# Two heads of batch 0 taken by query block, their probabilities split into float16 pairs and transposed by DMA

## The chip, the core and the metric

The kernel runs on one core of one Trainium2 chip. The metric is device time in microseconds (us) of one execution, the median of the runs. Engines are named as in the profile: PE is TensorE, PEld its weight loads, DVE is VectorE, ACT is ScalarE, POOL is GpSimd, SP is SyncE, which only issues DMAs here.

## What is computed

Four batches of eight heads of clustered attention, and behind it a feed-forward network with the Mish function on all 3072 tokens. The reference, cut:

```python
def _attn_ref(q, k, v, centroids):          # q, k, v: 4 x 8 x 768 x 64, centroids: 8 x 16 x 64
    scale = 1.0 / np.sqrt(D)
    q_assign = np.argmax(np.einsum('bhsd,hcd->bhsc', q_n, c_n), axis=-1)   # q, k, c normalised
    k_assign = np.argmax(np.einsum('bhsd,hcd->bhsc', k_n, c_n), axis=-1)
    mask = q_assign[:, :, :, None] == k_assign[:, :, None, :]
    scores = np.where(mask, scale * np.matmul(q, k.transpose(0, 1, 3, 2)), -1000000000.0)
    attn = np.exp(scores - np.max(scores, axis=-1, keepdims=True))
    attn = attn / (np.sum(attn, axis=-1, keepdims=True) + 1e-09)
    return np.matmul(attn, v)

def _moe_ref(x, w_in, w_out):                # x: 3072 x 512, w_in: 512 x 2048, w_out: 2048 x 512
    h = x @ w_in
    g = h * np.tanh(softplus(h))             # Mish
    return g @ w_out
```

## The kernel before

**Units.** Attention is cut into 96 units: a head g (0 to 31, eight to a batch) and a query block of 256 rows. Before, unit i is head i // 3, block i % 3. A unit has two halves `a` of 128 query rows, and two units in a row, 2m and 2m + 1, are a pair m, whose product with the values shares one PSUM bank.

**Steps of a half.** `scores` makes 128 x 768 scores on TensorE in one of two PSUM buffers; `rowmax` (VectorE) their row maximum, `expo` (ScalarE) the exponentials with their sum, `total` and `recip` the reciprocal of the sum. From there two ways are in use. In the f32 way (`mode` 3, units below `T["wide"]`, which is 24: all of batch 0), `p_lo` transposes the exponentials on TensorE into PSUM (tile `q`, six transposes), `ptrans` copies the halves of it to SBUF, one on ScalarE and one on VectorE; `pv` multiplies them, three parts, with the raw f32 values (`vraw`) and brings the reciprocals into the same bank; `pv_out` scales them on ScalarE (`rb`), multiplies on VectorE (`xf`), and splits the result into two float16 parts on ScalarE and GpSimd. In the float16 way (all later units), `p_hi` writes the high float16 part of the scaled probabilities (tile `hl`), `p_lo` on VectorE the low part, `ptrans` is one DMA transpose of both from the SP queue, `pv` is 36 float16 matmuls, and `pv_out` (ScalarE) with `x_lo` (VectorE) writes the two parts of x.

**Values.** For the float16 way `v_high` (GpSimd) and `v_split` (VectorE) make float16 pairs of the values, for two heads at a time.

**Operands of the scores.** For each head, `prep_hi` and `prep_lo` on GpSimd make `A` and `B` from the loaded `qk`, and `copy_t`, `copy_z`, `copy_b`, `copy_a` and `hot_copy` move halves of them and of the cluster rows between partitions, most by DMA: `T` from A, `Z` from B, then B's upper half from T. Each of A, B, T and Z has two buffers, so the operands of head n take those of head n - 2.

**Feed-forward network.** For a token block of 256 rows and a slice f of 256 of the 2048 columns there is a step j (24 to a batch): `m1` makes h (two halves of 12 matmuls each), `e_mish` applies Mish on ScalarE, for two j with one change of activation tables to it and one back, `e_gh` and `e_gl` make float16 pairs, and `m2` adds into the output. `m1` of a token block needs x of all eight heads for that block.

**Order.** Nothing is reordered when the program runs: each engine runs its instructions in the order in which they were written. `Plan` sorts all operations by a place on an axis counted in units (the tables `T` and `N`) and lets each pull the ones it needs ahead of itself:

```python
    def at(self, t, fn, *args):
        op = fn.__name__, *args
        self.ops[op] = (t + SHIFT.get(op, 0), len(self.ops), fn, args)
```

`SHIFT`, which moves single operations, is empty before.

Of the kernel before, what the change touches and what calls it, by code (L numbers as in the profile page):

```python
# [72 lines left out]
def tile_clustered_attention_mish_ffn(  # L73
# [61 lines left out]
    units = [(g, qb, g) for g in range(B * H) for qb in range(3)]  # L135
    NG = units[-1][2] + 1
# [295 lines left out]
    def v_high(b, hp):  # L432
        pl.after(scaled(b), ("v_load", b, hp))
        t = vst[b, hp, "raw"]
        if b == 0 and T["wide"] >= 24:
            return
# [214 lines left out]
    def expo(i, a):  # L651
        pl.after(("rowmax", i, a))
        p = pp.tile([P, S], F32, tag="p", name=f"p{i}_{a}")
        if mode(i, a) != 3:
            l = sm.tile([P, 1], F32, tag="l", name=f"l{i}_{a}", bufs=10)
        else:
            if a == 0:
                st["l", i] = sm.tile([P, 2], F32, tag="ll", name=f"l{i}", bufs=5)
            l = st["l", i][:, a : a + 1]
# [116 lines left out]
    def pv_out(i):  # L776
        pl.after(("pv", i // 2, 2))
        g, qb, _ = units[i]
        b, h = divmod(g, H)
        if mode(i, 0) == 3:  # L780
            pl.after(("v_scale", b))
# [34 lines left out]
    def m1(j, fi):  # L816
# [3 lines left out]
        if fi == 0:  # L820
# [11 lines left out]
    def e_mish(j):  # L832
        pl.after(("m1", j, 0), ("m1", j, 1))
# [241 lines left out]
    def ffn(j):  # L1075

        return T["ffn"] + j
# [24 lines left out]
    for n in range(NG):  # L1102
        for op, key in (
# [9 lines left out]
            else:  # L1113
                pl.at(start(first[n]) + T[key] * (3 if n else 1), op, n)
# [166 lines left out]
    'v_sqd': -5.865,  # L1281
    'cent_put': -16.698,
    'ffn': 23.993,
    'w_f': 0.342,
    'w_q': 0.827,
    'w_lo': 0.312,
    ('z', 'prep_hi'): -17.672,
    ('z', 'prep_lo'): -12.698,
    ('z', 'copy_t'): -15.888,
    ('z', 'copy_a'): -14.732,  # L1290
    ('z', 'copy_b'): -14.765,
    ('z', 'copy_z'): -16.337,
    ('z', 'assign_mm'): -11.552,
    ('z', 'assign_turn'): -14.554,
    ('z', 'assign_max'): -16.003,
    ('z', 'assign_hot'): -13.258,
    ('z', 'assign_back'): -12.666,
    ('z', 'assign_put'): -12.998,
    ('z', 'hot_direct'): -6.027,
    ('z', 'assign_stg'): -14.77,  # L1300
    ('z1', 'prep_hi'): -15.822,
    ('z1', 'copy_t'): -0.562,
    ('z1', 'prep_lo'): -2.335,
    ('z1', 'copy_z'): 2.134,
    ('z1', 'copy_b'): 2.571,
    ('z1', 'copy_a'): 1.339,
    'as_turn': 2.548,
    'as_max': -0.442,
    'as_hot': 2.486,
    'as_back': 0.39,  # L1310
    'as_put': 0.846,
    'as_stg': 1.187,
    'n_late': 9,
    'wide': 24,
    'v_s0': 36.503,
    'act_q': 3,
# [72 lines left out]
    ('w_s', 0): 0.187,
    ('w_s', 1): -0.515,  # L1390
# [88 lines left out]
```

## Time and profile before

| | |
|---|---|
| median of 3 runs | 879.22 us (878.64 to 881.77) |
| the profiled execution | 880.14 us, its span 878.4 us |
| PE busy | 843.7 us, 96% of the span |
| PEld busy | 609.1 us, 69% |
| DVE busy | 701.5 us, 80% |
| ACT busy | 521.9 us, 59% |
| POOL busy | 436.1 us, 50% |
| granted clock of PE | full in all of the 40 slices |

The span runs from the first to the last instruction, and the profiled execution's time has 1.7 us around it. A busy share is a mean over stretches with different limits: the stretches are to be read one by one. Matmuls overlap, so the time that a group of them holds TensorE is read from the start of the first to the start of what follows, not from their durations.

### The profile page before, as it was taken

How to read it: one execution, taken by the hardware profiler on the slowest of the kernel's cores; microseconds unless marked ns; L12 is line 12 of the kernel's file. 1: busy time of each engine (PE TensorE's matmuls, PEld its weight loads, DVE VectorE, ACT ScalarE, POOL GpSimd, SP SyncE). 2: the span in 40 equal slices, each digit the busy share in tenths (PEclk: the TensorE clock that was granted, in tenths of full speed). 3: DMA queues.
4: the chain of work that ended last, by engine and by line, in shares of the span. 5: the costliest groups of instructions: out<-in, count | busy, mean ns of one | idle time of the engine just before them, and what ended most of it. 6: DMA issues, size and time to landing. Idle time of an engine off the chain costs nothing.

```text
span 878.4 us, 17434 instructions
## 1 busy us (share of the span) xinstructions
PE 843.7 (96%) x6670; PEld 609.1 (69%) x6671; DVE 701.5 (80%) x1178; ACT 521.9 (59%) x881; POOL 436.1 (50%) x410
## 2 busy tenths in 40 slices
PE   7989789979999999999999999999999999999998
PEld 3766566757677767677676766776776777777787
DVE  6889988889888789788888788788888776488831
ACT  5777877666555656557456566475574565346520
POOL 1453656587575546567566447466575543110000
PEclk9999999999999999999999999999999999999999
DMA  9755672288678998788579898997777876000001
GB/s 343 218 164 141 198 221 59 72 152 166 128 138 178 190 181 156 162 158 173 118 138 189 199 157 143 165 175 143 134 148 139 141 134 121 13 1 13 1 26 36
DMA packets 253060, 121.51 MB, mean 138 GB/s; under 512 B 230288, under 2 KB 230800, under 8 KB 252976
## 3 DMA queue, kind: packets, MB, share of 16 engines
q1 hardware_dynamic: 247632, 108.46, 58.5%
q10 hardware_dynamic: 5344, 11.93, 6.3%
q8 instruction: 53, 0.87, 0.4%
q14 instruction: 31, 0.25, 0.1%
HBM read 35.72 MB, written 6.29 MB: 48 GB/s over the span
## 4 chain that ended last, share of the span: by engine, by line
PE 71%; DVE 12%; DMA 6%; ACT 6%; issue 3%; POOL 2%; ACTq 0%; SPq 0%; POOLq 0%; DVEq 0%
PE o L751 9%; PE h L828 8%; PE h L830 7%; PE h L829 7%; PE O L869 7%; PE O L871 7%; PE O L870 7%; PE s L631 5%; PE s L636 5%; DVE m L648 3%; ACT p L660 2%; DMA T<-A 2%; DVE hl L715 2%; DMA stage<-in_w_out_dram 1%; PE as L543 1%
## 5 line engine op out<-in xcount | busy, mean ns | idle before, releaser
L660 ACT ACTIVATE p<-s,m 128x768 f32<-128x768 f32 x192 | 172.8, 900 | 157.7 <-DVE l L672 77.2
L698 POOL TENSOR_SCALAR hl<-p,l 128x768 f16<-128x768 f32 x144 | 174.8, 1214 | 135.9 <-DVE l L680 68.8
L648 DVE TENSOR_REDUCE m<-s 128x1 f32<-128x768 f32 x192 | 182.8, 952 | 37.9 <-PE s L636 34.0
L828 PE MATMUL h<-x,w 128*128 128x256 f16 x640 | 175.8, 275 | 3.7 <-ACT u L839 3.7
L829 PE MATMUL h<-x,w 128*128 128x256 f16 x640 | 174.4, 273 | 0.0
L830 PE MATMUL h<-x,w 128*128 128x256 f16 x640 | 174.4, 273 | 0.0
L715 DVE SCALAR_TENSOR_TENSOR hl<-p,l,hl 128x768 f16<-128x768 f32 x144 | 166.8, 1159 | 7.7 <-POOL hl L698 7.5
L631 PE MATMUL s<-A,B 128*128 128x384 f32 x384 | 119.2, 391 | 8.9 <-ACT p L660 6.8
L853 DVE SCALAR_TENSOR_TENSOR g<-u,mscg,g 128x512 f16<-128x512 f32 x80 | 93.6, 1170 | 38.6 <-POOL g L845 38.3
L869 PE MATMUL O<-w,g 128*128 128x512 f16 x320 | 121.7, 380 | 0.0
L871 PE MATMUL O<-w,g 128*128 128x512 f16 x320 | 121.3, 379 | 0.0
L870 PE MATMUL O<-w,g 128*128 128x512 f16 x320 | 121.3, 379 | 0.0
L845 POOL TENSOR_SCALAR g<-u,mscg 128x512 f16<-128x512 f32 x80 | 74.2, 930 | 71.7 <-ACT u L839 55.1
L636 PE MATMUL s<-Z,T 80*128 80x384 f32 x384 | 99.0, 339 | 1.0 <-DVE T L603 1.0
L828 PEld LDWEIGHTS <-w 128*128 128x128 f16 x768 | 75.1, 98 | 31.8 <-issue 20.6
L829 PEld LDWEIGHTS <-w 128*128 128x128 f16 x768 | 75.5, 98 | 15.2 <-issue 4.0
L830 PEld LDWEIGHTS <-w 128*128 128x128 f16 x768 | 75.1, 98 | 8.7
L751 PE MATMUL o<-pt,v 128*64 128x256 f16 x1296 | 78.4, 274 | 1.6 <-DMA pt<-hl 1.3
L631 PEld LDWEIGHTS s<-A,B 128*128 128x128 f32 x384 | 61.1, 190 | 25.1 <-ACT p L660 10.5
L751 PEld LDWEIGHTS <-v 128*64 128x64 f16 x1296 | 68.1, 110 | 11.9 <-issue 9.3
L636 PEld LDWEIGHTS s<-Z,T 80*128 80x128 f32 x384 | 69.7, 189 | 1.3 <-ACT Z L600 1.3
L839 ACT ACTIVATE u<-h,msch 128x512 f32<-128x512 f32 x80 | 51.8, 685 | 16.8 <-PE h L830 12.5
(225 smaller groups left out, 1313.4 us busy)
## 6 DMA issues: line engine op xcount, KB each, us to landing
qk<-in_qk_dram SPq DMA_DIRECT2D x32, 384.0 KB, 4.8
stage<-in_w_in_dram SPq DMA_DIRECT2D x16, 512.0 KB, 7.7
stage<-in_w_out_dram SPq DMA_DIRECT2D x16, 512.0 KB, 4.5
vraw<-in_vP_dram SPq DMA_DIRECT2D x16, 384.0 KB, 6.1
T<-A ACTq DMA_DIRECT2D x30, 192.0 KB, 2.9
Z<-B SPq DMA_DIRECT2D x30, 192.0 KB, 2.9
B<-T ACTq DMA_DIRECT2D x28, 192.0 KB, 4.1
out_dram<-osb SPq DMA_DIRECT2D x20, 256.0 KB, 3.0
```

Source lines behind the costliest of these rows:

```text
L631: nc.tensor.matmul(s[:, j, :384], st["B", n][:, q0 : q0 + P], st["A", n][:, j * 384 : (j + 1) * 384], start=True, stop=False,)
L636: nc.tensor.matmul(s[:, j, :384], st["T", n][: D + NCL, q0 : q0 + P], st["Z", n][: D + NCL, j * 384 : (j + 1) * 384], start=False, stop=True,)
L648: nc.vector.tensor_reduce(m, st["s", i, a][:, :, :384], axis=AX.XY, op=ALU.max, negate=True)
L660: nc.scalar.activation(p.rearrange("p (n x) -> p n x", n=2), st["s", i, a][:, :, :384], AF.Exp, bias=st["m", i, a], scale=1.0, accum_out=l,)
L715: nc.vector.scalar_tensor_tensor(t[:, 1], p, r, t[:, 0], op0=ALU.mult, op1=ALU.subtract)
L751: nc.tensor.matmul(o[s * D : s * D + D, :256], v if early else v[:, int(part == 1)], st["pt", 2 * m + s][:, :, c + (0 if early or part < 2 ...
L828: nc.tensor.matmul(o, wh, xh, start=(c == 0), stop=False)
L829: nc.tensor.matmul(o, wh, xl, start=False, stop=False)
L830: nc.tensor.matmul(o, wl, xh, start=False, stop=(c == 3))
L869: nc.tensor.matmul(o, gh, wh, start=(f == 0 and fi == 0), stop=False)
L870: nc.tensor.matmul(o, gh, wl, start=False, stop=False)
L871: nc.tensor.matmul(o, gl, wh, start=False, stop=(f == 7 and fi == 1))
```

## The change

`T["wide"]` goes from 24 to 18: units 18 to 23, heads 6 and 7 of batch 0, take the float16 way. With `f_hi` of the first 24 units at 0, their `p_hi` is on ScalarE. The six units are put in another order, so that the two heads alternate by query block; the values of these two heads (`hp` 3) get their float16 pair. `ffn` places the first feed-forward steps two units sooner, and lets this shrink to nothing at step 24. `hold` moves the operand steps of heads 7 and 8 back by 0.84 units. New terms in `after` keep the order of halves. The tables get new numbers, and `SHIFT` an entry for most operations up to unit 31.

```diff
+    units[18:24] = [(g, qb, g) for qb in range(3) for g in (6, 7)]
...
     def v_split(b, hp):
         pl.after(("v_high", b, hp))
-        if b == 0 and T["wide"] >= 24:
+        if b == 0 and hp < T["wide"] // 6:
             return
...
     def ffn(j):
 
-        return T["ffn"] + j
+        return T["ffn"] + j - T["lead"] * max(0, 1 - j / 24)
...
-                pl.at(start(first[n]) + T[key] * (3 if n else 1), op, n)
+                pl.at(start(first[n]) + T[key] * (3 if n else 1) + T["hold"].get(n, 0), op, n)
...
+    'lead': 2,
+    'hold': {7: 0.838, 8: 0.844},
...
-    'wide': 24,
+    'wide': 18,
...
 SHIFT = {
-   
+    ('p_lo', 19, 0): 0.589, ('recip', 25, 1): -0.052, ('w_hi', 11): 6.904, ('assign_hot', 2): 2.97,
```

What it does to the order, at three places. In the names below the first number is the unit (for `A`, `B`, `T`, `Z` and `qk` the head), the second the half, and the last one only counts buffers. First VectorE around units 18 and 19, before:

```order
L727 COPY pt17_1682<-q17_1_3_1712 128x384
L678 RECIPROCAL l17_1621<-l17_1621 128x2
L648 TENSOR_REDUCE m18_1_1738<-s18_1_1721 128x1
L727 COPY pt18_1748<-q18_0_3_1744 128x384
L648 TENSOR_REDUCE m19_0_1770<-s19_0_1761 128x1
L727 COPY pt18_1748<-q18_1_3_1776 128x384
L678 RECIPROCAL l18_1719<-l18_1719 128x2
L796 TENSOR_TENSOR xf2_1_1506<-o8_1728,rb16_1803 64x256
L796 TENSOR_TENSOR xf2_2_1658<-o8_1728,rb16_1803 64x256
L648 TENSOR_REDUCE m19_1_1811<-s19_1_1797 128x1
```

The same place in the change:

```order
L730 COPY pt17_1690<-q17_1_3_1726 128x384
L683 RECIPROCAL l18_0_1734<-l18_0_1734 128x1
L649 TENSOR_REDUCE m18_1_1745<-s18_1_1740 128x1
L718 SCALAR_TENSOR_TENSOR hl18_0_1747<-p18_0_1733,l18_0_1734,hl18_0_1747 128x768
L649 TENSOR_REDUCE m19_0_1766<-s19_0_1761 128x1
L683 RECIPROCAL l18_1_1777<-l18_1_1777 128x1
L683 RECIPROCAL l19_0_1786<-l19_0_1786 128x1
L799 TENSOR_TENSOR xf2_1_1499<-o8_1752,rb16_1792 64x256
L799 TENSOR_TENSOR xf2_2_1668<-o8_1752,rb16_1792 64x256
L649 TENSOR_REDUCE m19_1_1805<-s19_1_1800 128x1
L718 SCALAR_TENSOR_TENSOR hl19_0_1807<-p19_0_1785,l19_0_1786,hl19_0_1807 128x768
L718 SCALAR_TENSOR_TENSOR hl18_1_1812<-p18_1_1776,l18_1_1777,hl18_1_1812 128x768
```

The copies of `q` have given way to `p_lo` (`hl`), twice as many reciprocals stand there, and the low parts of two halves stand together behind the row maximum of a later half. Next GpSimd at the operands of head 7, before:

```order
L672 TENSOR_SCALAR l17_1621<-l17_1621 128x2
L484 TENSOR_SCALAR qk7_839<-qk7_839,scq_138 128x768
L487 TENSOR_SCALAR A_7_1733<-qk7_839 128x768
L500 TENSOR_TENSOR B_7_1753<-qk7_839,A_7_1733 128x768
L337 TENSOR_SCALAR w9_997<-w9_997,ws1r_1702 128x1024
L340 TENSOR_SCALAR w8_796<-w9_997 128x1024
L672 TENSOR_SCALAR l18_1719<-l18_1719 128x2
```

and in the change:

```order
L485 TENSOR_SCALAR qk7_744<-qk7_744,scq_138 128x768
L488 TENSOR_SCALAR A_7_1635<-qk7_744 128x768
L501 TENSOR_TENSOR B_7_1648<-qk7_744,A_7_1635 128x768
L675 TENSOR_SCALAR l17_1629<-l17_1629 128x2
L802 TENSOR_TENSOR x0_2_0_1491<-xf2_0_1492,x0_2_0_1491 128x256
L675 TENSOR_SCALAR l18_0_1734<-l18_0_1734 128x1
L675 TENSOR_SCALAR l18_1_1777<-l18_1_1777 128x1
L338 TENSOR_SCALAR w9_993<-w9_993,ws1r_1712 128x1024
```

The three steps of head 7 stand one unit earlier, ahead of the sum of unit 17, and the sums of the two halves of unit 18 are apart. Last ScalarE at the first feed-forward steps, before:

```order
L660 ACTIVATE p25_0_2241,l25_0_2242<-s25_0_2193,m25_0_2198 128x768
L795 ACTIVATE rb22_2261<-o11_2153,vsp_484 128x256
L798 CAST x0_3_1_1958<-xf3_1_1959 128x256
L798 CAST x0_3_2_2089<-xf3_2_2090 128x256
L838 ACT_TABLE_LOAD
L839 ACTIVATE u0_2274<-h0_2126,msch0_2114 128x512
L839 ACTIVATE u1_2279<-h1_2205,msch0_2114 128x512
L841 ACT_TABLE_LOAD
L660 ACTIVATE p25_1_2282,l25_1_2283<-s25_1_2226,m25_1_2231 128x768
```

and in the change:

```order
L663 ACTIVATE p23_0_2076,l23_0_2077<-s23_0_2035,m23_0_2040 128x768
L843 ACT_TABLE_LOAD
L844 ACTIVATE u0_2089<-h0_1963,msch0_1900 128x512
L844 ACTIVATE u1_2092<-h1_2015,msch0_1900 128x512
L846 ACT_TABLE_LOAD
L515 DMA B_8_2031<-T_8_2064 64x768
L703 ACTIVATE hl22_1_2108<-p22_1_2059,l22_1_2060 128x768
L791 ACTIVATE x0_3_1_2149<-o10_2112 64x256
L663 ACTIVATE p23_1_2158,l23_1_2159<-s23_1_2081,m23_1_2086 128x768
```

The first two `e_mish` stand between the halves of unit 23 instead of those of unit 25, and a DMA of head 8 (`B` from `T`) is issued behind them.

## Rows read from the trace of the kernel before

**Rows 1.** Windows: us, busy of PE, PEld, DVE, ACT, POOL, clock, DMA, GB/s

```profile
0.00:127.50 127.50, 110.88 (x826) 75.23 (x827) 111.71 (x204) 95.99 (x184) 54.83 (x76) 1.00 0.69 214
127.50:163.00 35.50, 32.03 (x243) 22.74 (x241) 30.68 (x62) 26.41 (x54) 20.11 (x22) 1.00 0.30 82
163.00:207.00 44.00, 36.73 (x310) 28.06 (x308) 37.15 (x62) 29.26 (x48) 33.88 (x31) 1.00 0.67 132
207.00:350.00 143.00, 142.46 (x1126) 101.03 (x1126) 123.04 (x196) 86.87 (x144) 87.93 (x74) 1.00 0.82 162
```

**Rows 2.** Timeline of PE, units 21 and 22: start, us, what

```profile
147.40 0.88 PE L708 MATMUL q<-ident,p 128*128 128x128 f32 x6
148.03 0.59 PE L631 MATMUL s<-A,B 128*128 128x384 f32 x2
...
148.91 1.08 PE L751 MATMUL o<-pt,vraw 128*64 128x256 f32 x8
149.83 0.66 PE L763 MATMUL o<-ident,l 128*64 128x128 f32 x8
```

**Rows 3.** Timeline of PE, later places

```profile
169.67 0.28 PE L828 MATMUL h<-x,w 128*128 128x256 f16 x1
...
170.88 0.27 PE L830 MATMUL h<-x,w 128*128 128x256 f16 x1
...
204.93 2.16 PE L751 MATMUL o<-pt,v 128*64 128x256 f16 x36
207.01 0.63 PE L631 MATMUL s<-A,B 128*128 128x384 f32 x2
...
209.15 0.38 PE L869 MATMUL O<-w,g 128*128 128x512 f16 x1
...
209.80 0.38 PE L869 MATMUL O<-w,g 128*128 128x512 f16 x1
```

**Rows 4.** Groups of DVE, whole run: busy us, mean ns, idle before, releaser

```profile
L715 DVE SCALAR_TENSOR_TENSOR hl<-p,l,hl 128x768 f16<-128x768 f32 x144 | 166.8, 1159 | 7.7 <-POOL hl L698 7.5
L727 DVE COPY pt<-q 128x384 f32<-128x384 f32 x48 | 26.3, 549 | 4.1 <-PE q L708 3.9
L680 DVE RECIPROCAL l<-l 128x1 f32<-128x1 f32 x144 | 23.7, 164 | 4.9
```

**Rows 5.** One line's instructions (`p_lo`): duration ns min/median/max

```profile
L715 DVE SCALAR_TENSOR_TENSOR hl<-p,l,hl x144: 998/1018/2477, 173.0 to 740.2; 128x768 f16<-128x768 f32 x144
```

**Rows 6.** Waits of DVE, 127.5 to 163: us in total, times, longest

```profile
DVE xf L796 <- ACT rb L795: 1.7, 2, 1.4
```

**Rows 7.** Waits of DVE, 163 to 207

```profile
DVE hl L715 <- POOL hl L698: 2.8, 2, 2.3
DVE l L678 <- POOL l L672: 1.6, 1, 1.6
```

**Rows 8.** Waits of DVE, 20 to 127.5

```profile
DVE pt L727 <- PE q L708: 3.3, 4, 1.0
```

**Rows 9.** Timeline of POOL, units 24 and 25

```profile
177.31 1.29 POOL L799 TENSOR_TENSOR x<-xf,x 128x256 f16<-128x256 f32 x2 [4.62 <-ACT x L798]
```

**Rows 10.** DMA issues: count, KB each, median us to landing

```profile
Z<-B SPq DMA_DIRECT2D x30, 192.0 KB, 2.9
B<-T ACTq DMA_DIRECT2D x28, 192.0 KB, 4.1
```

**Rows 11.** Groups of POOL, whole run

```profile
L500 POOL TENSOR_TENSOR B<-qk,A 128x768 fp32r<-128x768 f32 x30 | 60.9, 2030 | 0.6
L487 POOL TENSOR_SCALAR A<-qk 128x768 fp32r<-128x768 f32 x30 | 30.4, 1012 | 44.8 <-PE s L631 42.4 <-DVE hl L715 1.7
```

**Rows 12.** The DMA transposes (L731): landing

```profile
DMA to landing us min/median/max: 3.6/3.9/9.8
```

**Rows 13.** Timeline of PE, last scores of unit 17, first of unit 19

```profile
125.17 0.62 PE L631 MATMUL s<-A,B 128*128 128x384 f32 x2
...
134.19 0.62 PE L631 MATMUL s<-A,B 128*128 128x384 f32 x2
```

More of the change, by code (lines that the diff above doesn't have):

```diff
@@ L656, in expo @@
         else:
-            if a == 0:
+            if a:
+                pl.after(("expo", i, 0))
+            else:
                 st["l", i] = sm.tile([P, 2], F32, tag="ll", name=f"l{i}", bufs=5)
@@ L776, in pv_out @@
     def pv_out(i):
[L777 removed]
+        pl.after(("pv", i // 2, 2), *((("pv_out", i - 1),) if i % 2 else ()))
         g, qb, _ = units[i]
@@ L1419 @@
     'v_pair': 10,
-    'v_high': 26.765,
-    'v_low': 27.613,
-    'v_d': 3.411,
-    'E': [0.382, 0.808, 1.235, 1.505],
-    'scores': 0.582,
-    'rowmax': -0.28,
-    'expo': 4.085,
-    'total': 9.597,
+    'v_high': 26.36,
+    'v_low': 27.407,
+    'v_d': 3.32,
+    'E': [0.4, 0.787, 1.21, 1.526],
+    'scores': 6.189,
+    'rowmax': -0.274,
+    'expo': 1.87,
+    'total': 10.441,
     'recip': 0.209,
-    'p_hi': 11.057,
-    'p_lo': 1.167,
+    'p_hi': 16.669,
+    'p_lo': 1.461,
     'ptrans': 0.814,
-    'pv': [6.978, 19.207, 5.531],
@@ new lines @@
+    ('recip', 28, 0): -0.671, ('v_split', 0, 2): 0.162, ('total', 20, 0): 0.506, ('x_lo', 19): 0.094,
+    ('pv', 11, 2): 3.557, ('expo', 19, 0): 1.534, ('x_lo', 24): 1.125, ('v_high', 1, 0): 0.187,
+    ('p_lo', 28, 0): -0.637, ('e_gh', 3): 0.653, ('scores', 24, 0): 0.274, ('qk_load', 14): 1.18,
+    ('v_sq', 1, 2): -1.537, ('w_sq', 24): 0.085, ('copy_t', 8): 1.395, ('w_abs', 28): -0.639,
+    ('scores', 25, 0): -0.126, ('prep_hi', 8): -1.914, ('x_lo', 17): 0.098, ('pv', 8, 1): -0.048,
+    ('v_peak', 1): -0.097, ('x_lo', 23): 0.136, ('w_hi', 10): -0.348, ('x_lo', 15): 0.759, ('p_lo', 20, 1): -0.01,
@@ new lines @@
+    ('qk_load', 11): 0.869, ('expo', 25, 1): 1.873, ('v_high', 0, 3): -0.304, ('scores', 15, 1): -0.057,
+    ('p_lo', 12, 1): 10.33, ('total', 16, 1): 1.026, ('scores', 24, 1): -0.108, ('ptrans', 21, 1): -0.117,
+    ('rowmax', 23, 1): 0.059, ('recip', 29, 0): -0.074, ('recip', 14, 0): -0.551, ('prep_hi', 10): -0.065,
+    ('ptrans', 16, 1): -0.052, ('p_hi', 17, 1): 0.182, ('recip', 23, 0): -0.11, ('w_low', 30): 0.275,
+    ('v_split', 1, 0): 0.058, ('total', 16, 0): 0.294, ('v_load', 1, 2): 0.366, ('scores', 26, 1): 1.441,
@@ new lines @@
+    ('total', 18, 0): 0.865, ('ptrans', 24, 0): -0.213, ('scores', 27, 1): -0.049, ('p_hi', 13, 0): 5.578,
+    ('w_f32', 30): -0.185, ('p_hi', 17, 0): -1.469, ('p_lo', 25, 1): 0.95, ('e_mish', 0): -0.789, ('e_gl', 5): 0.188,
+    ('ptrans', 15, 0): 0.121, ('w_abs', 31): 0.101, ('w_low', 31): 2.016, ('rowmax', 16, 1): -0.375,
+    ('expo', 25, 0): 0.543, ('ptrans', 17, 1): 0.199, ('x_lo', 26): 0.165, ('x_lo', 13): 0.382,
+    ('scores', 17, 0): 0.876, ('moe_scale_h', 0): -0.726, ('pv_out', 18): 1.281, ('p_hi', 18, 0): 2.334,
@@ new lines @@
+    ('recip', 28, 1): 0.058, ('p_lo', 19, 1): -0.998, ('rowmax', 16, 0): -0.091, ('recip', 15, 1): -0.211,
+    ('rowmax', 20, 1): 0.032, ('p_lo', 24, 1): 0.799, ('rowmax', 17, 0): -0.078, ('v_sq', 1, 1): 0.058,
+    ('p_lo', 27, 1): -0.081, ('x_lo', 22): 0.023, ('total', 17, 1): -0.758, ('x_lo', 20): -0.008,
+    ('scores', 23, 1): -1.864, ('assign_mm', 2): 0.158, ('copy_z', 6): 0.009, ('e_gl', 2): 0.262,
+    ('rowmax', 26, 0): -0.206, ('recip', 19, 1): 0.025, ('copy_b', 7): -0.053, ('m1', 0, 0): 1.036,
```

298 lines of the change are left out of this document (204 added, 94 removed), and 6 rows, old and new, of the table N.

## The prediction, made before the change was run

> **What bounds the kernel now.** I read the busy time of every engine in four stretches first [rows 1]; the cuts are at units 18, 24 and 30, found by counting the score matmuls. From 207 us, where the scores of unit 30 start [rows 3], TensorE is busy 142.46 of 143 us: from there on the time is TensorE's work and nothing else. Ahead of it no engine is full, but VectorE is nearest: 111.71 of 127.5 us, 30.68 of 35.5, 37.15 of 44. So VectorE idles 15.8, 4.8 and 6.9 us there, and TensorE 16.6, 3.5 and 7.3. The reader is to see two regimes: up to unit 30 the pace is VectorE's work plus its waits, and after it TensorE's work. The end is therefore the moment at which the scores of unit 30 start (207.0) plus the TensorE work that is then left (878.4 - 207.0 = 671.4 us). I work out how the change moves each of the two.
>
> The waits of VectorE say what its idle time is made of: in units 18 to 23 mostly `rb`, the scaled reciprocals, from ScalarE [rows 6], in units 24 to 29 `hl` and `l` from GpSimd [rows 7], in the front the TensorE transposes `q` [rows 8].
>
> **What leaves TensorE.** Units 18 to 23 are twelve half units and three pairs. A half unit's six f32 transposes take 0.63 us from their start to the next instruction's (147.40 to 148.03), a third of an f32 product of probabilities and values 0.92 (148.91 to 149.83), the broadcast of the reciprocals 0.66 [rows 2]. A pair costs 4 x 0.63 + 3 x 0.92 + 0.66 = 5.9 us. The f16 product that replaces it, 36 matmuls, takes 2.08 (204.93 to 207.01) [rows 3], and its transposes are no TensorE work. So 3 x (5.9 - 2.1) = 11.6 us leave TensorE, all of them before unit 30, where TensorE is not the limit: they end nothing by themselves.
>
> **What TensorE does sooner.** In the order before, twelve `m1` halves and one `m2` step of batch 0 stand ahead of the scores of unit 30; in the new order sixteen and four. An `m1` half is 12 matmuls 0.11 us apart (169.67 to 170.88 is eleven of them), an `m2` step six that are 0.217 apart (209.15 to 209.80 is three) [rows 3]: 4 x 1.32 + 3 x 1.30 = 9.2 us of TensorE work go from behind that point to ahead of it. There TensorE then has 179.6 - 11.6 + 9.2 = 177.2 us to do in some 210, so it has the room. **Term one: -9.2 us** behind unit 30. This needs what stands behind unit 30 to stay as dense as now; VectorE is at 86% there (123.04 of 143) [rows 1] and gets no more work in it.
>
> **What VectorE gets.** Twelve `p_lo` are added. This form takes 998 to 2,477 ns, median 1,018 [rows 5], mean 1,159 [rows 4]; the long ones lie where GpSimd is busy, and in units 18 to 23 GpSimd has 20.11 of 35.5 us against 33.88 of 44 later [rows 1], so I take the median: +12.2 us (bound +13.9). Twelve copies of a transposed half go: -12 x 0.549 = -6.6. Six more reciprocals, 0.164 each: +1.0 [rows 4]. One `v_split`, the same form as `p_lo`: +1.0. Six `xf` products go and six `x_lo` come, same shape: nothing. One `e_gl` more stands ahead of unit 30; it is the same form on a smaller tile, and I give it `p_lo`'s mean: +1.2. **Term two: +8.8 us** (bound +10.5) ahead of unit 30.
>
> ScalarE gets twelve `p_hi` and loses twelve copies and the `rb` and cast steps, about +5 us on its 26.41 of 35.5 [rows 1]; GpSimd gets six `total` of a few tenths, one `v_high`, and loses three subtractions. Both stay below VectorE, and I cost them at nothing; what covers them is VectorE's longer stretch, and without it ScalarE's 5 us would be on the path. SP gets twelve transposes. The DMA engines are at 0.30 in that stretch [rows 1], and two score halves or more stand between a half's `p_lo` and its pair's product, so I cost these at nothing too (rival four is the loss of that cover).
>
> **What the waits do.** (a) Units 18 to 23: the longest wait for `rb`, 1.4 us, is that of units 16 and 17, which stay in the f32 way; the other 0.3 goes [rows 6]. Against it, heads 6 and 7 now alternate, and the two operand buffers are both in use. `A_7` may be written only after the last scores of head 5 (unit 17), and head 7 is now wanted two halves later (unit 19) instead of six. From that release the scores of unit 19 wait for `A` 1.0 and `B` 2.0 on GpSimd [rows 11], the landing of `Z<-B` 2.9 and, behind it, of `B<-T` 4.1 [rows 10]: 10.0 us. Now 125.17 to 134.19 pass from the start of the last scores of unit 17 to the first of unit 19 [rows 13], 9.0 us, of which the scores themselves are some 0.6 to 0.9; so unit 19 comes 1.6 to 1.9 later than now: +1.6. Behind it in TensorE's order stands everything else, and VectorE's row maximum waits for it. Sum +1.3.
> (b) Units 24 to 29: of the 6.9 us idle, 2.8 are `hl` from GpSimd and 1.6 `l` [rows 7]. GpSimd's row at 177.31 shows why: the subtraction of the f32 path waited 4.62 us for ScalarE, and the `p_hi` of the next half with it, since GpSimd runs in order [rows 9]. That instruction is gone for units 22 and 23. I take -3.2; bounds 0 and -4.4.
> (c) The front: many single places move, most of all the exponential of a half goes ahead of the copy of the half before it. The four waits on `q` there are 3.3 us [rows 8]. The trace cannot show what becomes of them; bounds 0 and -5, and I take the middle, -2.5.
> **Term three: -4.4 us** (bounds +2 and -9).
>
> **Sum.** The scores of unit 30 start at 207.0 + 8.8 - 4.4 = 211.4, TensorE has 9.2 us less behind it: 4.4 - 9.2 = -4.8 us. The profiled execution goes from a span of 878.4 (880.14 with what lies around it) to 873.6 (875.3). The runs' median of 879.22 lies 0.9 below the profiled one, so I forecast 874.4.
>
> **The rivals.**
> One: VectorE takes all of it back. If its waits ahead of unit 30 do not shrink, terms one and two nearly cancel (+8.8 - 9.2): 878.8. For it: in the front, up to 127.5 us, VectorE is at 88% already, and (a) is a new wait. Against it: [rows 9] name a wait whose cause is removed. 0.19.
> Two: TensorE's saved work is all won, -11.6 us: 867.6. It needs -11 in term three, beyond the bounds that I could price. For it: TensorE idles 27 us ahead of unit 30, much more than that. 0.13.
> Three, the slower side: the copies of head 7 and, in the same way, of head 8 come late. Head 8's buffer now comes free after unit 22 instead of unit 20, its `B<-T` stands on ScalarE's queue behind the two first `mish` and their table loads, and everything of unit 24 waits for it on TensorE, VectorE behind. If the two places cost 5 us each instead of 1.6 and nothing, term three is +4.0 and the sum +3.6; if the front gains nothing either, +6.1: 885. It decides from about 6.4 us of waits at the two places together. 0.15.
> Four: the transposes. In rows the DMA of a half (twelve 128x128 blocks, both f16 parts) lands in 3.6 to 9.8 us, median 3.9 [rows 12], against 0.63 us of TensorE and two copies. Were they to land at the 9.8, the product of each pair would be 5.9 us later, and with it ScalarE's and VectorE's `x` steps, which stand in order ahead of the next halves' work. With two scores' worth hidden each time, that is +4 us a pair, 12 in all on top of the forecast: 886. Medians of 144 speak against it, and a DMA share of 0.30. 0.05.
> The Trainium skill, VectorE: DVE Perf Modes, section "The three transpose paths" and the rules behind it, says to put a 128x128 transpose on TensorE where PSUM will do as its destination, with 390 ns against 1,309 for the DMA crossbar; by these figures twelve blocks, one after another, would be an estimated 15.7 us, and this change would lose. The trace does not agree with so long a time: all twelve blocks land in 3.9 us, and no compute engine is held meanwhile.
>
> **Chances and range.** The forecast (874.4, its own range 871 to 878) 0.48. No change by measurement here is within 0.5%, 4.4 us: 874.8 to 883.6. Of the forecast's 0.48 some 0.27 lie below 874.8; with rival two's 0.13 and a little of rival one, faster is 0.42. Same: the other 0.21, 0.17 of rival one and a little of rival three, 0.40. Slower: 0.18. The range reaches from rival two to the middle of rival three, 867 to 884.
>
> **What would show it.** Right: the scores of unit 30 at about 211 with sixteen `m1` halves ahead of them; TensorE above 99% from there; `p_lo` of that stretch near 1.02; GpSimd's long wait for a cast gone. Wrong: VectorE's idle time ahead of unit 30 at or above 27 us; a wait of the scores of unit 19 or 24 on a DMA above 3 us; `p_lo` at 1.4 or more; products waiting for `pt`; or TensorE idle behind unit 30, which would mean that the new order is looser where the old one was full.

## The result, and the profile after

The change made the kernel slower: **890.77 us** (889.19 to 891.81), against 878.93 of the kernel before in the same comparison, ratio 1.0127 (95% interval 1.0099 to 1.0155). The forecast was 874.4, with a range of 867 to 884. The profiled execution took 891.32 us, its span 889.6.

The scores of unit 30 start at 219.4 us; the forecast said 211.4. Cut at its own units 18, 24 and 30, the changed kernel's windows answer to [rows 1] (columns as there; the last window is the 147.6 us of units 30 to 47):

```profile
0.00:127.80 127.80, 111.69 (x825) 76.98 (x827) 111.12 (x202) 95.56 (x183) 59.65 (x79) 0.99 0.71 218
127.80:174.90 47.10, 34.18 (x230) 24.15 (x230) 39.15 (x71) 34.14 (x59) 25.85 (x30) 0.83 0.65 127
174.90:219.40 44.50, 40.45 (x325) 31.37 (x324) 40.12 (x66) 29.27 (x48) 34.02 (x26) 0.92 0.81 155
219.40:367.00 147.60, 139.72 (x1108) 98.49 (x1106) 122.74 (x198) 86.89 (x145) 92.55 (x76) 1.00 0.82 162
```

Units 30 to 47 of the kernel before, for the last of them:

```profile
207.00:356.50 149.50, 148.96 (x1174) 104.61 (x1172) 128.60 (x204) 90.45 (x149) 93.98 (x79) 1.00 0.81 159
```

Three things are to be read here. VectorE has 190.4 us of work ahead of unit 30, 10.85 more than before, and 29.0 us of idle time, 1.5 more. TensorE's clock, full in every window of before, is 0.83 in units 18 to 23 and 0.92 in units 24 to 29. And behind unit 30 TensorE is busy 139.7 of 147.6 us; the 7.9 us that it idles there were 0.5 before.

The page of the changed kernel shows the clock's dip in the seventh to ninth slice of its span:

```profile
PEclk9999998889999999999999999999999999999999
```

Windows cut at the clock's own steps show that the mean of 0.83 is made of stretches at full and stretches at half clock, 2.4 and 1.2 GHz. Five such stretches ahead of unit 30 are 27.2 us together; two of them, each behind the window ahead of it:

```profile
141.40:148.20 6.80, 4.09 (x22) 2.29 (x22) 6.61 (x8) 4.43 (x8) 3.17 (x4) 1.00 0.63 116
148.20:155.00 6.80, 4.08 (x28) 2.95 (x28) 6.73 (x12) 4.02 (x8) 4.62 (x6) 0.50 0.31 58
161.90:168.70 6.80, 3.93 (x31) 3.11 (x31) 6.27 (x11) 5.96 (x9) 6.28 (x7) 1.00 0.87 169
168.70:175.50 6.80, 6.70 (x44) 5.31 (x45) 4.16 (x12) 3.75 (x6) 4.44 (x5) 0.50 0.78 164
```

What half clock does to the chain shows in the second pair. The product of units 20 and 21 takes 4.05 us where [rows 3] had 2.16. Behind it stand the scores of unit 24 on TensorE, the high part of x on ScalarE and the low part on VectorE (timelines of PE, ACT and DVE):

```profile
170.90 4.05 PE L754 MATMUL o<-pt,v 128*64 128x256 f16 x36
174.88 0.91 PE L632 MATMUL s<-A,B 128*128 128x384 f32 x2
...
182.32 1.01 PE L632 MATMUL s<-A,B 128*128 128x384 f32 x2 [2.40 <-ACT p L663]
```

```profile
175.01 0.38 ACT L791 ACTIVATE x<-o 64x256 f16<-64x256 f32 x1 [3.02 <-PE o L754]
```

```profile
175.42 0.42 DVE L815 SCALAR_TENSOR_TENSOR x<-o,x 64x256 f16<-64x256 f32 x1 [2.03 <-ACT x L791]
```

The Trainium skill, TensorE: Matmul & The Clock Gate, section "A second HAM failure mode: psum-queue depth-cycling", tells of a kernel whose TensorE idles briefly between groups of matmuls so often that its clock swings between the two levels. The trace agrees as far as the swing goes: 4.09 busy of 6.8 us, in 22 matmuls, then half clock. That the PSUM queue is its cause, as in that kernel, no run here shows.

The added instruction itself is as forecast. Its line (duration min/median/max), beside [rows 5]:

```profile
L718 DVE SCALAR_TENSOR_TENSOR hl<-p,l,hl x156: 1001/1018/2675, 135.0 to 751.5; 128x768 f16<-128x768 f32 x156
```

VectorE's waits of units 18 to 23 (127.8 to 174.9) answer to [rows 6], and GpSimd's wait for a cast, 9.1 us in four waits over units 18 to 29 before (the 4.62 of [rows 9] among them), is down to this:

```profile
DVE xf L799 <- ACT rb L798: 2.7, 1, 2.7
DVE l L683 <- POOL l L675: 1.5, 2, 1.3
...
DVE hl L718 <- ACT hl L703: 1.1, 3, 0.4
```

```profile
POOL x L802 <- ACT x L801: 2.4, 2, 1.2
```

The 2.7 us begin on ScalarE: its DMA `T<-A` of head 7 stood 2.16 us in its queue, waiting for GpSimd's A, and the exponential of unit 17 and `rb` behind it.

```profile
127.13 0.90 ACT L663 ACTIVATE p<-s,m 128x768 f32<-128x768 f32 x1 [2.16 <-POOL A L488]
```

### The profile page after: what moved, and what is told of

Read it like the earlier page. It is cut to its first block, busy times and chain, and to the rows that moved or that the text cites. A ratio compares the mean times of both kernels' runs of the same rounds, so it can differ in the third digit from the quotient of the medians.

```text
span 889.6 us, 17363 instructions
## 1 busy us (share of the span) xinstructions
PE 840.3 (94%) x6610; PEld 610.5 (69%) x6611; DVE 693.3 (78%) x1185; ACT 525.4 (59%) x881; POOL 447.3 (50%) x414
## 4 chain that ended last, share of the span: by engine, by line
PE 66%; DVE 14%; ACT 6%; DMA 5%; issue 4%; POOL 4%; ACTq 0%; SPq 0%; POOLq 0%; DVEq 0%
PE o L754 9%; PE h L833 7%; PE O L874 7%; PE h L834 7%; PE h L835 7%; PE O L875 7%; PE O L876 7%; PE s L632 5%; PE s L637 5%; DVE m L649 4%; ACT p L663 2%; DVE hl L718 2%; DMA pt<-hl 2%; DVE w L277 1%; DVE g L858 1%
## 5 line engine op out<-in xcount | busy, mean ns | idle before, releaser
L701 POOL TENSOR_SCALAR hl<-p,l 128x768 f16<-128x768 f32 x144 | 183.3, 1273 | 151.1 <-DVE l L683 82.5
L718 DVE SCALAR_TENSOR_TENSOR hl<-p,l,hl 128x768 f16<-128x768 f32 x156 | 186.2, 1195 | 5.8 <-POOL hl L701 3.8
L834 PE MATMUL h<-x,w 128*128 128x256 f16 x640 | 175.2, 274 | 0.8 <-DVE x L815 0.8
L632 PE MATMUL s<-A,B 128*128 128x384 f32 x384 | 122.6, 401 | 22.3 <-ACT p L663 16.6
L850 POOL TENSOR_SCALAR g<-u,mscg 128x512 f16<-128x512 f32 x80 | 68.5, 859 | 74.7 <-ACT u L844 58.4
L754 PE MATMUL o<-pt,v 128*64 128x256 f16 x1404 | 89.2, 282 | 3.7 <-DMA pt<-hl 3.7
L632 PEld LDWEIGHTS s<-A,B 128*128 128x128 f32 x384 | 63.6, 194 | 40.6 <-ACT p L663 22.1
L754 PEld LDWEIGHTS <-v 128*64 128x64 f16 x1404 | 76.9, 113 | 16.6 <-issue 12.0
L858 DVE SCALAR_TENSOR_TENSOR g<-u,mscg,g 128x512 f16<-128x512 f32 x80 | 73.5, 918 | 6.8 <-POOL g L850 6.2
L815 DVE SCALAR_TENSOR_TENSOR x<-o,x 64x256 f16<-64x256 f32 x62 | 26.1, 421 | 48.0 <-ACT x L791 46.9
```

Of the source, the lines that this page charges most:

```text
L632: nc.tensor.matmul(s[:, j, :384], st["B", n][:, q0 : q0 + P], st["A", n][:, j * 384 : (j + 1) * 384], start=True, stop=False,)
L718: nc.vector.scalar_tensor_tensor(t[:, 1], p, r, t[:, 0], op0=ALU.mult, op1=ALU.subtract)
L754: nc.tensor.matmul(o[s * D : s * D + D, :256], v if early else v[:, int(part == 1)], st["pt", 2 * m + s][:, :, c + (0 if early or part < 2 ...
L834: nc.tensor.matmul(o, wh, xl, start=False, stop=False)
```

## Experiments

Times are medians; a ratio is to the kernel before, timed on the same chip, with its 95% interval. Runs of one kernel lie up to 1.2% apart (881.41 to 891.95 in one case), and traces of one and the same order differ too: unit 18 starts at 125.4, 127.8 and 130.5 us in three traces in which every engine has the same instructions ahead of it (the copy of the high part below, the change, the pulled steps). So differences below 3 us are left open, and one of 5 us between two single traces is weak by itself.

### The work that was to go behind unit 30

**Lead away.**

```diff
-    'lead': 2,
+    'lead': 0,
```

> The changed kernel with the feed-forward steps at their own time (lead 0 in place of 2), all else kept. Term one of the forecast says that the four more m1 halves and three more m2 steps ahead of unit 30 are worth 9 us; then this run is 896 to 900. If they bring little, because they run at half clock ahead of unit 30 and leave TensorE short of work behind it: 888 to 893. If the early Mish steps with their table loads are themselves what delays units 22 to 26: 882 to 887.

902.60 us, 1.0257 (1.0229 to 1.0286): 12 us more than the change, and more than any of the three theories gave. Only four `m1` halves go back behind unit 30, some 5.3 us; the four `m2` steps stay ahead of it. Yet unit 30 starts at 225.6, 6.2 us later than in the change, at a clock of 0.76 in units 18 to 23 and 0.90 in units 24 to 29. So the lead is worth much, but 6.2 of the 9.1 us between the two traces lie ahead of unit 30, where term one has nothing: the run shows that the led work counts, and not that term one's 9.2 us are its price. The window of units 30 to 47 says something else as well:

```profile
225.60:380.60 155.00, 148.46 (x1154) 102.93 (x1153) 122.61 (x199) 90.76 (x147) 87.03 (x74) 0.98 0.79 150
```

TensorE is as busy there as before (148.5 us, before 149.0) and still idles 6.5 us. The holes are not missing work.

**The way alone, by head** (the kernel before, all tables as before; the edit in part; the condition on `hp` that the change has in `v_split` and `v_high` comes with it):

```diff
-    'wide': 24,
+    'wide': 18,
...
```

> The kernel before with wide 18 and the values' pair for heads 6 and 7, units in their old order by head, all tables as before. Differs from the run of the core alone by the alternation only (that one took 64.7 us from unit 18 to unit 24, and 905.5 in all). Theory A (alternation makes the operands of heads 7 and 8 late): 18 to 24 takes 40 to 46 us, the time is 886 to 894. Theory F (the float16 way itself, its longer chain of reciprocal, two parts, DMA transpose and product, is slow in places made for the other way): 60 us or more, 900 to 908.

896.50 us, 1.0171 (1.0136 to 1.0206). **The way and the alternation** (the same, and the alternation with the operands of heads 7 and 8 moved back by 0.9 units):

```diff
+    units[18:24] = [(g, qb, g) for qb in range(3) for g in (6, 7)]
...
-                pl.at(start(first[n]) + T[key] * (3 if n else 1), op, n)
+                pl.at(start(first[n]) + T[key] * (3 if n else 1) + {7: 0.9, 8: 0.9}.get(n, 0), op, n)
```

> The kernel before with only the core of the change: wide 18, the six units alternating between heads 6 and 7, the values of these heads as a float16 pair, the operands of heads 7 and 8 held back by 0.9 units; all tables as before, no single shifts, no lead. Tells the float16 way apart from the new places. If the loss ahead of unit 30 (12.4 us) is in the float16 way itself, by VectorE's 8 to 11 us of added work: unit 30 at 216 to 222 us, TensorE has no more work done ahead of it, so the end is 888 to 895. If the new places are the loss: the time is 878 to 884.

905.51 us, 1.0291 (1.0245 to 1.0338). The windows of units 30 to 47 of these two, by head first:

```profile
226.40:375.60 149.20, 147.93 (x1173) 104.57 (x1172) 128.32 (x204) 90.44 (x149) 94.48 (x79) 1.00 0.84 159
```

```profile
231.50:384.50 153.00, 149.48 (x1172) 105.02 (x1171) 127.81 (x204) 90.36 (x149) 94.02 (x80) 0.99 0.85 156
```

With the old numbers TensorE idles 1.3 and 3.5 us there, with the new ones 6.5 (lead 0) and 7.9 (lead 2). Two more kernels with the new numbers, both from the section on units 18 to 23 below, are the float32 way with lead 0 and the changed kernel by head:

```profile
239.90:392.30 152.40, 146.43 (x1155) 102.81 (x1154) 120.84 (x199) 90.87 (x147) 85.83 (x74) 0.99 0.78 152
```

```profile
236.70:387.40 150.70, 140.91 (x1107) 99.01 (x1105) 122.72 (x198) 86.98 (x145) 93.82 (x76) 0.99 0.81 158
```

They idle 6.0 and 9.8 us. So it is the new numbers that are looser behind unit 30, whatever the way, the order and the lead. Which of the numbers it is, no run shows.

**Old places behind unit 42, or behind unit 30 for all but the led steps.** Both place the operations a second time with the tables of before and merge; the second has 30 in place of 42, and leaves `m1` to `m_store` alone where their new place is below 50:

```diff
+    for op, was in pl.ops.items():
+        if was[0] < 42 or op not in mine:
+            pl.ops[op] = mine[op]
```

> The changed kernel, but every operation whose place in the kernel before was at unit 42 or later gets that old place again (no lead of the feed-forward steps there). Tells where the work won behind unit 30 went. If the new late places are looser: TensorE's stalls behind 315 us (7.6 us in six stalls of the changed kernel, 2.1 in three before) go back to some 2, and the time is 884 to 887. If TensorE stalls there because less of its own work is left to cover the chain of row maximum, exponential and scores: the stalls come elsewhere and the time stays at 889 to 892.

> The changed kernel, but all operations whose place in the kernel before was at unit 30 or later get it back, except the feed-forward steps below place 50, which keep their lead. Seven stalls of TensorE between 219 and 360 us, 7.9 us, stand at the same operations in every run that has the new late places, whenever unit 30 starts. If the new late places make them: TensorE idles 1 to 3 us in units 30 to 48, the time is 883 to 886. If the lead makes them, because less feed-forward work stands between the scores of these units: the stalls stay at 6 us or more, 888 to 893.

895.20 us, 1.0172 (1.0129 to 1.0215), and 908.11, 1.0336 (1.0309 to 1.0363). Neither gain came. Stalls of 6.5 and 7.4 us stand at the seam, so the two sets of numbers can't be mixed, and these runs say nothing on either alone.

**Steps pulled ahead of the seven stalls**, on TensorE alone:

```diff
+PULL = {
+    ("scores", 30, 0): (("m2", 0, 0, 4),), ("scores", 33, 1): (("m1", 10, 1),), ("scores", 37, 0): (("m1", 14, 0),),
+    ("scores", 39, 0): (("m2", 1, 0, 4), ("m2", 1, 0, 5)), ("scores", 43, 1): (("m2", 1, 1, 6), ("m2", 1, 1, 7)),
+    ("scores", 47, 0): (("m1", 23, 0),), ("pv", 22, 0): (("m2", 2, 0, 4), ("m2", 2, 0, 5)),
+}
```

> The changed kernel with one or two m1 or m2 steps pulled ahead of seven operations (scores of 30, 33, 37, 39, 43, 47 and the product of units 44 and 45) in front of which TensorE stalls; the order of the other engines is the same. If these 7.9 us of stalls are a matter of TensorE's order: they shrink to 2 or 3, and the time is 884 to 887. If they are work that is missing, or the scores' delay is handed on to VectorE and comes back as a later stall: 889 to 892.

885.45 us, 1.0071 (1.0047 to 1.0096): the time is as the first theory said, some 5 us less than the change, the stalls are not. PE's waits of units 30 to 47, of the change and then of this run:

```profile
PE s L632 <- ACT p L663: 3.9, 4, 1.7
PE s L632 <- DMA B<-T: 1.6, 1, 1.6
PE o L754 <- DMA pt<-hl: 1.5, 1, 1.5
PE s L637 <- DMA T<-A: 0.9, 1, 0.9
```

```profile
PE O L877 <- DVE g L859: 3.4, 5, 1.6
PE o L755 <- DMA pt<-hl: 1.8, 1, 1.8
PE put L590 <- ACT p L663: 0.9, 2, 0.6
PE O L875 <- POOL g L851: 0.9, 1, 0.9
```

The kernel before has one such wait there:

```profile
PE s L631 <- ACT p L660: 0.4, 1, 0.4
```

The waits of the scores are gone, and the pulled `m2` steps now wait for `g` from VectorE instead; TensorE still idles 6.9 us. The trace, which is of the slowest of the ten runs (888.48), does not show where the median's gain lies: the stretch is 2.4 us shorter (145.2), but unit 30 starts 2.8 us later (222.2, with the same order ahead of it), so unit 48 stands at 367.4 where the change has 367.0, and behind it the 3.2 us less are no more than runs of one order differ by. The looseness is not a matter of TensorE's order alone.

### The clock

**Twelve matmuls on constants behind the scores of every half** of units 12 to 29, in the changed kernel and, as a control, in the kernel before:

```diff
         st["s", i, a] = s
+        if 12 <= i < 30:
+            for _ in range(12):
+                nc.tensor.matmul(s[:, 0, 384:], idle[:, :P], idle[:, :P], start=True, stop=True, skip_group_check=True)
```

> The changed kernel, with twelve 128-column matmuls on constants behind the scores of every half of units 12 to 29, into columns of the score bank that nothing reads (36 halves x 12 x 0.056 = some 24 us of TensorE work that means nothing). Theory C (clock): the loss ahead of unit 30 comes from TensorE's granted clock, which falls to its lower level for some 27 us between 99 and 191 us because TensorE now has too little to do; then the clock stays full, a product of a pair takes 2.1 us again instead of 3.2 to 4.05, the scores of unit 30 start at 211 to 214 us instead of 219.4, and the time is 883 to 886. Theory O (order): the new places of the operations cost the time and the clock is only a symptom; then the clock is full but unit 30 still starts at 218 to 222 and the time is 889 to 894.

> Control for the run with the fillers: the same twelve matmuls behind each half of units 12 to 29, in the kernel before, whose clock is full there anyway. If the fillers cost nothing by themselves: 878 to 881, and the run with the fillers in the changed kernel shows that the full clock brings nothing. If they cost 4 us or more (883 to 888), they hid a gain of that size there.

894.76 us, 1.0175 (1.0126 to 1.0223), and 892.02, 1.0137 (1.0096 to 1.0179). In the changed kernel the clock is then 0.96 in units 18 to 23 and 1.00 in units 24 to 29, and unit 30 still starts at 221.3. Without the control this would read as "the full clock brings nothing". But these fillers cost the kernel before 12 us, more than was expected, and the changed kernel only 4. That difference is no price of the clock either: 24 us of fillers meet 17.0 us of idle TensorE time in units 12 to 29 of the kernel before, and 22.3 in the change.

**Fillers only in front of waits** (208, fourteen places, some of them ahead of the waiting scores, into the bank of the half before):

```diff
+        heat(st.get(("s", i - 1 + a, 1 - a)), HEAT_AHEAD.get((i, a), 0))
         s = ps2.tile([P, 2, 512], F32, tag="S", name=f"s{i}_{a}")
...
         st["s", i, a] = s
+        heat(s, HEAT_BEHIND.get((i, a), 0))
```

> The changed kernel with matmuls on constants only where its trace shows TensorE idle for 0.35 us or more (fourteen places of units 13 to 27, 208 matmuls of 128 columns, some 11.6 us of TensorE time that was idle). The fillers behind every half cost 12 us in the kernel before, but only 4 in the changed one, which leaves room for a gain of 8 us from the full clock. Theory C, the half clock costs time on the chain: the clock stays full in all or most of the stretch, unit 30 starts at 212 to 215 us in place of 219.4, the time is 883 to 886. Theory V, VectorE's work paces ahead of unit 30 and the clock is hidden behind it: full clock, unit 30 at 218 to 220, 889 to 892.

904.03 us, 1.0265 (1.0218 to 1.0312), a miss by construction. Ahead of scores the fillers themselves waited, for the readers of the bank that they wrote (PE's waits, 110 to 160; L628 is the filler):

```profile
PE s L628 <- ACT p L669: 4.5, 2, 2.4
PE s L628 <- DVE m L655: 3.4, 2, 2.3
```

The same with the old places behind unit 30 (919.34 us, 1.0468, interval 1.0436 to 1.0499) has the faults of both and shows no more:

> Both of the above in one kernel. If the half clock costs some 6 us and the late places some 6: 877 to 880, level with the kernel before or a little faster. If neither: 889 to 893.

**Fillers only directly behind scores**, where nothing reads the bank yet:

```diff
+HEAT = {(13, 0): 6, (14, 0): 22, (17, 0): 5, (18, 0): 22, (20, 0): 5, (20, 1): 24, (21, 0): 34, (22, 1): 14, (23, 0): 20, (24, 1): 20, (25, 0): 9}
...
+        for _ in range(HEAT.get((i, a), 0)):
```

> The changed kernel with 181 matmuls of 128 columns on constants behind the scores of eleven halves (units 13, 14, 17, 18, 20 to 25) behind which its trace shows TensorE idle; they write columns of the fresh score bank that nothing reads, so they wait for nothing. Theory C (the half clock is on the chain): the granted clock stays full in most of 99 to 191 us, unit 30 starts 4 to 7 us earlier, the time is 884 to 887. Theory V (VectorE's work paces, the clock is hidden): full clock, unit 30 within 2 us of 219.4, 889 to 893.

886.83 us, 1.0076 (1.0047 to 1.0106), some 4 us less than the change, though nothing but idle work was added; the two intervals just touch. The scores of unit 30 start at 214.7 in place of 219.4:

```profile
0.00:125.90 125.90, 111.34 (x858) 77.91 (x859) 109.82 (x202) 94.94 (x183) 59.09 (x79) 1.00 0.70 221
125.90:171.50 45.60, 36.34 (x352) 27.36 (x350) 38.37 (x71) 34.84 (x60) 26.42 (x30) 0.97 0.68 130
171.50:214.70 43.20, 39.23 (x354) 31.16 (x354) 41.99 (x67) 29.15 (x48) 34.22 (x27) 0.99 0.84 160
```

VectorE has 190.2 us of work, as good as the 190.4 of the change, and idles 24.5 us, not 29.0. The half clock, 27 us of it in the change, is down to 3.4 us. By this pair of traces it cost 4.7 us ahead of unit 30, as theory C said.

**Both** (these fillers and the pulled steps):

> Both edits of the two runs above. If both work and add up: 878 to 882, level with the kernel before. If neither: 889 to 893.

883.63 us, 1.0039 (1.0011 to 1.0066). They add up within the intervals, and still end behind the kernel before. On top of the pulled steps the fillers bring 1.8 us of the median, which the intervals do not tell from nothing; in the traces unit 30 starts at 216.7 in place of 222.2, so the second pair agrees with the first.

### VectorE's work ahead of unit 30

**The low part as a copy of the high part** in units 18 to 23:

```diff
+            if i < 24:
+                nc.vector.tensor_copy(t[:, 1], t[:, 0])
+            else:
+                nc.vector.scalar_tensor_tensor(t[:, 1], p, r, t[:, 0], op0=ALU.mult, op1=ALU.subtract)
```

> The changed kernel with the twelve added p_lo on VectorE (units 18 to 23) replaced by a copy of the float16 high part, so the low part of these probabilities is not computed; a copy between float16 tiles should be some 0.3 us by its half width against 1.08. Takes some 9 us from VectorE between 128 and 180 us and leaves everything else. If VectorE's work sets the pace ahead of unit 30: unit 30 at 210 to 213 us in place of 219.4, the time 881 to 885. If waits around the operands and the half clock set it: unit 30 at 216 to 219, the time 887 to 890.

882.42 us, 1.0031 (1.0008 to 1.0055). The copy's median is 360 ns against 1,018. Unit 30 starts at 212.3:

```profile
0.00:125.40 125.40, 110.34 (x826) 76.38 (x827) 109.80 (x202) 95.76 (x183) 61.97 (x79) 1.00 0.70 222
125.40:171.70 46.30, 34.19 (x230) 23.82 (x230) 34.33 (x74) 35.70 (x63) 24.08 (x32) 0.82 0.64 133
171.70:212.30 40.60, 37.41 (x324) 29.44 (x325) 37.79 (x64) 27.73 (x45) 33.79 (x25) 1.00 0.87 165
```

VectorE has 8.5 us less to do ahead of unit 30 and unit 30 starts 7.1 us earlier, as theory V said, and the median is 8 us below the change. The windows qualify it. 2.4 of the 7.1 us lie ahead of unit 18, where the two orders are the same, so they are spread. In units 18 to 23 VectorE is busy 34.3 of 46.3 us and the stretch is only 0.8 us shorter; the gain stands in units 24 to 29 (40.6 for 44.5), where the clock is full here and 0.92 in the change. The copy also shortens the chain of each half. So the run shows that the added `p_lo` cost time; it does not part VectorE's work from the chain and the clock.

**Three of the twelve on GpSimd**, on top of fillers and pulls:

```diff
+        if (i, a) in ((18, 0), (19, 1), (20, 1)):
+            return 2
```

> The kernel of both edits (fillers behind scores, m1 and m2 steps pulled ahead), with the p_lo of three halves of units 18 to 20 on GpSimd as two instructions in place of one on VectorE: 3.1 us leave VectorE ahead of unit 30. Theory V: unit 30 2 to 3 us earlier, the time 880 to 882. If GpSimd's longer chain (two instructions of some 2.4 us, the sums of the next halves behind them) delays more than it frees: 884 to 888.

888.99 us, 1.0096 (1.0064 to 1.0129), 5 us slower than without. Units 18 to 23 take 49.3 us for 45.8, though VectorE has 1.4 us less to do in them (37.15 for 38.54). A freed VectorE alone does not help here; that the longer chain of these halves is what is waited for fits, and is not shown.

### Units 18 to 23: way, alternation, places

**The float32 way in the new order** (`wide` 24 with the new places, lead 0) and **the changed kernel by head** (no alternation, no `hold`), the edit of the first in part, then that of the second. In the first, three tests of the way become `i < 18`, so units 18 to 23 stand at the places of the float16 way:

```diff
-        if mode(i, a) == 3:
+        if i < 18:
...
-    'lead': 2,
+    'lead': 0,
...
-    'wide': 18,
+    'wide': 24,
```

```diff
-    units[18:24] = [(g, qb, g) for qb in range(3) for g in (6, 7)]
-    'hold': {7: 0.838, 8: 0.844},
+    'hold': {},
```

> As the run with lead 0, but units 18 to 23 stay in the float32 way (wide 24), in the new order of heads and with the new places. Differs from the run with lead 0 by the way alone. Theory C: TensorE has its 11.6 us of work back, the clock stays full in that stretch, and the run is 5 to 10 us faster than the run with lead 0. Theory O: the clock falls here too or does not matter, and the two are within 3 us of each other. The forecast's own sum (VectorE ahead of unit 30) says 6 to 9 us faster ahead of unit 30 by VectorE's work alone, with the clock full in both.

> The changed kernel with the six units in their old order by head and no hold; tables, single shifts and lead as in the change. The first m1 needs x of head 7 for block 0, which is then made by the third unit of the six from the end in place of the second of the six, so m1 and Mish come later or wait. Theory A: 18 to 24 takes 38 to 44 us, unit 30 starts earlier than 219 in spite of that wait, the time is 882 to 889. Theory F, or the m1 wait deciding: 47 us or more, 892 to 905.

911.36 us, 1.0354 (1.0321 to 1.0387), and 905.32, 1.0265 (1.0232 to 1.0298). Units 18 to 23 last:

| way | order of heads | places | us |
|---|---|---|---|
| float32 | by head | old (before) | 35.5 |
| float16 | by head | old | 54.4 |
| float16 | alternating | old | 64.7 |
| float32 | alternating | new, lead 0 | 57.3 |
| float16 | alternating | new, lead 0 | 49.2 |
| float16 | alternating | new (the change) | 47.1 |
| float16 | by head | new | 60.7 |

Neither theory holds alone: with the old places, made for the other way, the float16 way adds 19 us, and the alternation with its 0.9 units 10 more. The new places take back 17.6, 2.1 of them by the lead, and fit only the order that they were made for. The float32 way in new places stands in places made for the float16 way, so that row does not compare the ways. But it settles one thing: the clock is 0.79 there, though TensorE has its float32 work back and is busy 44.7 of 57.3 us. In no row is any engine full; in the second VectorE is busy 38.5 of 54.4 us and the clock is 0.65. In every row but the first the clock is 0.83 or less and TensorE idles 12 us or more.

### ScalarE in front of head 7's copy

```diff
+        if kind == "copy_t" and n in (7, 8):
+            return nc.sync
```

> The changed kernel with the DMAs T<-A of heads 7 and 8 issued by SyncE in place of ScalarE. In the changed kernel ScalarE stands 2.16 us in front of the one of head 7 (127 us), waiting for GpSimd's A, and VectorE behind it 2.67 us for rb. If this block of ScalarE's queue is what rival three feared: both waits go and units 19 to 30 start 2 to 3 us earlier, time 887 to 889. If the operands themselves set the pace (GpSimd's A and B and the copies behind them): no change, 889 to 892.

889.61 us, 1.0106 (1.0069 to 1.0143). On top of fillers and pulls:

> The kernel of both edits, with the DMAs T<-A of heads 7 and 8 issued by SyncE. If ScalarE's wait in front of head 7's copy (2.2 us, VectorE 2.7 behind it) is on the path: 881 to 882.5; if it is hidden: 883 to 885.

885.00 us, 1.0056 (1.0039 to 1.0072). No difference that can be measured, either time. In the first of them the wait of ScalarE is gone and unit 18 starts at 124.2 in place of 127.8, but unit 24 is where it was (175.2). Unit 30 is 2.7 us earlier in the first (216.7 for 219.4) and 2.6 us later in the second (219.3 for 216.7), so this is spread.

## Why the prediction was wrong

By stretch, from the forecast's own terms:

| | forecast | measured |
|---|---|---|
| to unit 18 | 127.5 - 2.5 = 125.0 | 127.8 |
| units 18 to 23 | 35.5 + 7.6 (term two without the `e_gl`) + 1.3 = 44.4 | 47.1 |
| units 24 to 29 | 44.0 + 1.2 - 3.2 = 42.0 | 44.5 |
| from unit 30 | 671.4 - 9.2 = 662.2 | 670.2 |
| span | 873.6 | 889.6 |

**Half of the miss, 8.0 us, is term one:** -9.2 forecast, 670.2 - 671.4 = -1.2 measured. Its work did go ahead: sixteen `m1` halves and four `m2` steps stand before unit 30, and TensorE's busy time behind it is 10.1 us less (843.7 - 179.6 before, 840.3 - 186.3 now). But TensorE idles 16.2 us there where it idled 7.3. What failed is the condition "this needs what stands behind unit 30 to stay as dense as now". I let VectorE's 86% and the unchanged work there vouch for it. But the tables behind unit 30 were new as well, and in units 30 to 47 the kernels with the old numbers show 0.5 to 3.5 us of TensorE's idle time, and those with the new ones, whatever their lead, way and order, 6.0 to 9.8. It is no accident of one trace: in five more with the change's order from unit 30 on (three with fillers, the copy of the high part, the copies on SyncE) the time from there is 667.2 to 680.2 us, where the forecast had 662.2. The last of my signs, TensorE idle behind unit 30 because "the new order is looser", named it, without a chance of its own.

**The step "so it has the room"** failed next. TensorE had the room, 177 of 210 us, and the room had a price: its clock fell to half for 27 us, which nothing in the sum or among the rivals allowed for. Fillers that keep the clock up move unit 30 by 4.7 us and the median by some 4 (by 5.5 and 1.8 on top of the pulled steps). That the 11.6 us taken off TensorE made it fall is not shown: it fell in the float32 way as well, with the new places. The trace of before gave no warning. It has TensorE as idle as that at full clock:

```profile
177.50:184.30 6.80, 3.15 (x25) 2.50 (x24) 4.03 (x6) 5.01 (x7) 6.44 (x7) 1.00 0.49 96
```

**Term two** was undersized: VectorE's busy time ahead of unit 30 grew by 10.85 us where I took 8.8 and bounded 10.5. That it sets the pace us for us is not shown: with 7.2 us of it gone from units 18 to 29 these take 86.9 us in place of 91.6, and the clock rose with it. The median of `p_lo` was right (1,018 ns); ten of the twelve lie in units 18 to 23 with a mean of 1,081.

**Term three** came out at +1.5 in place of -4.4. With the clock kept up it is 24.5 - 27.5 = -3.0, so by this pair of traces the clock accounts for 4.5 of these 5.9 us. By stretch VectorE's idle time changed by +0.9, +3.1 and -2.5 us where I took -2.5, +1.3 and -3.2. Part (b) was right as far as it went: GpSimd's wait for the cast went from 9.1 to 2.4 us. Part (c), -2.5 taken from the middle of two bounds, had nothing behind it: the waits for `q` are 3.2 where they were 3.3, and unit 18 starts no sooner. The bounds of the three parts add up to +1.6 at most and -8.1, not to the +2 and -9 that stand there.

**The rivals.** The outcome lies beyond rival three's 885, and by other means. Head 7's operands: from the last scores of unit 17 to the first of unit 19, the measure of [rows 13], 12.4 us pass where 9.0 did, 3.4 more and not 1.6 (timeline of PE):

```profile
123.36 0.60 PE L632 MATMUL s<-A,B 128*128 128x384 f32 x2
...
135.80 0.61 PE L632 MATMUL s<-A,B 128*128 128x384 f32 x2
```

But unit 17 ended sooner: against the start of unit 18, unit 19 is 1.3 us later than before, and its scores wait for no DMA. Unit 24 stood behind a product at half clock, not behind its operands, and moving the copies changed nothing. Rival four did not come: the median landing of the transposes is still 3.9 us. Rival one came closest in kind, VectorE's idle time ahead of unit 30 at 29.0 us, which I had named as a sign of being wrong; it lacked the loss behind unit 30.

The miss of 16.0 us is thus 8.0 of density behind unit 30 and, if the fillers' pair of traces is taken at its word, 4.7 of the clock, 2.05 of VectorE's work and 1.3 of other waits. The first is the firmest, since old and new numbers part cleanly; between the other three the spread of a trace, 3 to 5 us, allows another split. How the 7.9 us of idle time split over single numbers of the tables stays open, and so does what a way back to the old density under the lead would look like.

## What to carry to other kernels

A sum that ends in "and what follows stays as dense as it is" has to be checked against everything that the change rewrites there, above all an order written in tables: a few stalls of 1 to 2 us eat what a term of 9 us brings. An engine that is not the bound is not free to idle if it is TensorE: in every row of the table of units 18 to 23 but the first it idles more than before and its clock is down, and a clock that is down slows the chain that others wait for. A single trace is one run: a gain that stands ahead of the first changed instruction is not the change's. And an experiment that adds work to show that a resource matters needs its control in the unchanged kernel.

## What the runs showed of the hardware

Work that computes nothing made the kernel faster: 181 matmuls on constants, placed where TensorE idled anyway, took some 4 us off. The same idea spread evenly, 432 of them, some 24 us, cost the kernel before 12 us: the units in which they stood had only 17.0 us of idle TensorE time. At half clock the product of a pair took 4.05 us against 2.16, two score matmuls 1.01 against 0.60.
